# Opening the product of w3 and w_out2 with three row blocks, and taking the norms' roots with ln and exp

## Chip, cores and metric

The kernel runs on one core of a Trainium2 chip. The metric is the device time of one execution in microseconds (us), the median over the runs shown.

## What is computed

Attention over 4 batches of 12 heads (448 positions, 64 wide), with q and k normalised by the root of their mean square, feeds two feed-forward blocks. The second block multiplies its gated activations by `w3` and then by `w_out`:

```python
def rmsnorm(x, g):
    rms = np.sqrt(np.mean(x * x, axis=-1, keepdims=True) + 1e-06)
    return x / rms * g
...
h = x @ w_in; x = np.maximum(h, 0.0) ** 2 @ moe_w_out      # first block, cut
...
a = x @ w1
b = x @ w2
h = a * b @ w3
return (h @ w_out).astype(np.float32)
```

Tokens: 1792; model width 768; widths 2048 in the first block and 1024 in the second. The weights come as float64, the rest as float32.

## The kernel before

**Heads and fill.** The main loop (line 676) goes through the 48 heads, one to four steps of attention work per head: scores (`stage_qk`, line 513), exponentials (`stage_exp`, 529), transposes (`stage_t`, 562), product with v (`stage_v`, 614), and preparation of later heads (`head_prep`, 474; `group_prep`, 437, once for every four heads). Between them `fill(n)` (line 648) draws about n matmuls from a generator of matrix work, six times a head. While the 12 heads of batch 0 run, the generator is `gen_w3o` (line 272): it multiplies w3 by w_out2 ahead of time, so that the second block needs one product fewer. Its 384 matmuls are spread evenly over 13 heads, 29.5 each (line 677). After that the generator is `gen_moe` for the batch just finished.

**The product.** `gen_w3o` goes through eight row blocks `ic` of w3, each for two halves of w_out2's columns (384 each). For one row block and half it adds up eight steps `jc`, three matmuls each (`mm3`, line 260: high times high, high times low, low times high part) in one accumulator of the three PSUM tiles "mm" (line 95), which ScalarE then copies out (line 287) to one of two tiles "osb" for a store to DRAM (line 289). The first row block needs all 8 blocks of w_out2's first half, then all 8 of its second half; these stay in SBUF (tiles "x", "act" and "x2") for all later row blocks.

**Units.** Every weight block is a unit, in the order of the list `units` (lines 121 to 141): a block of w_out2 is 128x384, half a row block of w3 is 128x512. The order is: first half of w3 row block 0, w_out2 half 0 blocks 0 to 3, second half of row block 0, w_out2 half 0 blocks 4 to 7, w_out2 half 1, and then the other row blocks. `advance` (line 240) takes each unit through these steps, a few units ahead of its use: load of the float64 words into one of four "raw64" tiles by SyncE's queue (line 180), high word by ScalarE (line 194), low word by GpSimd or ScalarE (lines 198 and 200), joining to float32 by VectorE (line 207), rounded high part by ScalarE (line 106), low part by GpSimd or VectorE (line 114).

**Norms.** `rsqrt` (line 425) takes an inverse root on VectorE: an integer estimate (line 428) and three rounds of three small instructions (lines 432 to 434). It is called three times for the first group of four heads and once for each of the other 11 groups.

**Order.** The program's order is a priority: a planner in the compiler sorts the instructions of every engine by it and by estimated times, and each engine, SyncE's queue of loads included, then goes through its list in order. In the opening that list on SyncE has the first group's loads with units 0 and 1 among them (`load_group`, lines 396 to 403), then q of head 1, then (by `load_head(2)`) q of head 2, v, and k and q of the second group.

Of the kernel before, what the change touches and what calls it, by code (L numbers as in the profile page):

```python
# [8 lines left out]
F32 = mybir.dt.float32  # L9
F32R = mybir.dt.float32r  # L10
# [4 lines left out]
ALU = mybir.AluOpType  # L15
# [14 lines left out]
def attention_moe_kernel(  # L30
# [22 lines left out]
    NE = w_out.shape[0] // 4  # L53
    KF = w_out.shape[2] // 64
    NJ = w1.shape[0] // 2
    NIC = w3t.shape[0] // 2
    HC = KX * 128 // 2
    ENGS = {"v": nc.vector, "g": nc.gpsimd}
    KCS = ((0, 128), (128, 128), (256, 128), (384, 64))
# [61 lines left out]
    units = []  # L121
    wo_at, w3_at = {}, {}

    def add_wo(half, g):
        for j in range(NIC // 2):
            jc = g * NIC // 2 + j
            wo_at[half, jc] = len(units)
            units.append((wo2[jc, half], None))

    def add_w3(i):  # L130
        w3_at[i] = len(units)
        units.append((w3t[i], None))

    add_w3(0)
    add_wo(0, 0)
    add_w3(1)
    add_wo(0, 1)
    add_wo(1, 0)
    add_wo(1, 1)
    for i in range(2, 2 * NIC):  # L140
        add_w3(i)
    U0 = len(units)
    wo_units = set(wo_at.values())
    def two_first(n, on=True):
# [72 lines left out]
    def split_hi(i):  # L217
        n = units[i][0].shape[-1]
        if i in wo_units:
            k = pos["wo"]  # L220
            pos["wo"] += 1
            p, nm = (xp, "x") if k < 2 else ((actp, "act") if k < 10 else (x2p, "x2"))
            t = p.tile([128, 2, S], F32R, name=nm, tag=nm)
        else:
            t = hlp.tile([128, 2, 512], F32R, name="hl", tag="hl")
        copy_on("a", t[:, 0, :n], raws[i][:, :n])
        hls[i] = t
# [27 lines left out]

    def use(u):
        advance(u)
        return hls.pop(u).rearrange("p a (k m) -> p a k m", m=128)

    def mm3(ps, w, wk, x, i, n):  # L260
        last = n - 1
# [4 lines left out]
    def hl_pair(t, n=S):  # L266
        return (t[:, 0, :n], t[:, 1, :n])
# [2 lines left out]
    wo = {}  # L270

    def gen_w3o():
        for ic in range(NIC):
            ws = None
            for half in range(2):
                ps = ps_mm.tile([128, 512], F32, name="mm", tag="mm")
                for jc in range(NIC):
                    if ws is None or jc * 2 // NIC >= len(ws):
                        ws = (ws or []) + [use(w3_at[2 * ic + len(ws or [])])]
                    if ic == 0:  # L280
                        advance(wo_at[half, jc])
                        wo[half, jc] = hls.pop(wo_at[half, jc])
                    w = ws[jc * 2 // NIC]
                    mm3(ps[:, :HC], w, jc % (NIC // 2), hl_pair(wo[half, jc], HC), jc, NIC)
                    yield 3
                o = t2.tile([128, S], F32, name="osb", tag="osb")
                copy_on("a", o[:, :HC], ps[:, :HC])
                k, c = divmod(ic, NIC // 2)
                nc.sync.dma_start(
                    out=w3o.rearrange("(e k) p (c m) -> e k p c m", k=2, m=128)[half * 3:half * 3 + 3, k, :, c, :]  # L290
                    .rearrange("e p m -> p e m"),
                    in_=o[:, :HC].rearrange("p (e m) -> p e m", m=128),
                )


    xs = {}
# [128 lines left out]
    def rsqrt(y, x):  # L425
        t = small.tile([P, 2, GH * C], F32, name="nt", tag="nt")
        t = t[:, :x.shape[1], :x.shape[2]]
        nc.vector.tensor_scalar(
            out=y.bitcast(I32), in0=x.bitcast(I32), scalar1=-0.5, scalar2=1597463007.0, op0=ALU.mult, op1=ALU.add
        )  # L430
        for _ in range(3):
            nc.vector.tensor_tensor(out=t, in0=y, in1=y, op=ALU.mult)
            nc.vector.scalar_tensor_tensor(out=t, in0=t, scalar=-0.5, in1=x, op0=ALU.mult, op1=ALU.mult)
            ins = nc.vector.scalar_tensor_tensor(out=y, in0=t, scalar=1.5, in1=y, op0=ALU.add, op1=ALU.mult)
        return ins.ins

    def group_prep(g):
# [220 lines left out]
    MOE = 3 * (NFC * KX + 2 * NE * KF + 2 * NJ * KX + NE * NIC)  # L658
    W3O = 3 * 2 * NIC * NIC

    nc.sync.dma_start(out=g_sb, in_=g_in)
    load_group(0)
    load_head(1)
    make_identity(nc, ident)
    nc.vector.tensor_copy(out=ident_r, in_=ident)
    nc.vector.scalar_tensor_tensor(
# [7 lines left out]
    start_fill(gen_w3o(), W3O)  # L674
    first.close()
    for h in range(NH + 1):
        n = W3O / ((H + 1) * 6) if h <= H else MOE / (H * 6)
        load_head(h + 3)
        load_v(h + 1)
        if h % GH == 0:  # L680
            load_group(h // GH + 1)
        stage_qk(h, 0)
        fill(n)
        stage_exp(h, 0)
        if h % H != 1:
            stage_x(h - 2)
        stage_t(h - 1, 0)
        stage_t(h - 1, 1)
        fill(n)
        stage_lo(h - 1)  # L690
        if h < NH:
            v_prep(h)
        fill(n)
        stage_k(h + 1)
        stage_t(h - 1, 2)
        stage_t(h - 1, 3)
        fill(n)
        stage_lo(h - 1)
        stage_qk(h, 1)
        fill(n)  # L700
        stage_exp(h, 1)
        fill(n)
        stage_v(h - 1)
        if h % GH == 1:
            group_prep(h // GH + 1)
        head_prep(h + 2)
        if h and h % H == 0:
            fill(1e9)
            stage_x(h - 1)
            start_fill(gen_moe(h // H - 1), MOE)  # L710
# [57 lines left out]
```

## Time and profile before

| | us |
|---|---|
| median of 3 runs | 1234.7 (1232.09 to 1235.27) |
| the profiled execution | 1234.55 |
| its span in the profile | 1232.8 |
| TensorE matmul busy (PE) | 1160.9, 94% |
| GpSimd busy (POOL) | 781.3, 63% |
| ScalarE busy (ACT) | 728.5, 59% |
| VectorE busy (DVE) | 709.7, 58% |

PE is the matmul side of TensorE and PEld its weight loads; SP is SyncE, whose queue starts the loads, and SPq its queue. Times in the rows are us from the start of the span. A line number is that of the instruction in the kernel; L106 and L114 are the helpers that copy and subtract, so there the names of the tiles tell what is done.

### The profile page before, as it was taken

How to read it: one execution, taken by the hardware profiler on the slowest of the kernel's cores; microseconds unless marked ns; L12 is line 12 of the kernel's file. 1: busy time of each engine (PE TensorE's matmuls, PEld its weight loads, DVE VectorE, ACT ScalarE, POOL GpSimd, SP SyncE). 2: the span in 40 equal slices, each digit the busy share in tenths (PEclk: the TensorE clock that was granted, in tenths of full speed). 3: DMA queues.
4: the chain of work that ended last, by engine and by line, in shares of the span. 5: the costliest groups of instructions: out<-in, count | busy, mean ns of one | idle time of the engine just before them, and what ended most of it. 6: DMA issues, size and time to landing. Idle time of an engine off the chain costs nothing.

```text
span 1232.8 us, 18950 instructions
## 1 busy us (share of the span) xinstructions
PE 1160.9 (94%) x6192; PEld 1049.3 (85%) x6192; DVE 709.7 (58%) x1314; ACT 728.5 (59%) x1553; POOL 781.3 (63%) x772
## 2 busy tenths in 40 slices
PE   3789999998989899999999999999999999999998
PEld 2578888886878789998998998999999999999998
DVE  6699879768978774646567555655664421012100
ACT  5889876767657565656645555656545554343342
POOL 5875534655676655766776764856766556678673
PEclk9999999999998999999999999999999999999999
DMA  7774557888888755555535455544544443333342
GB/s 218 244 238 151 165 146 226 276 283 264 251 264 257 234 180 179 146 148 145 151 118 161 139 169 158 143 142 127 154 123 120 138 138 113 107 116 102 104 125 75
DMA packets 111347, 207.63 MB, mean 168 GB/s; under 512 B 12208, under 2 KB 66704, under 8 KB 111248
## 3 DMA queue, kind: packets, MB, share of 16 engines
q1 hardware_dynamic: 107792, 200.92, 54.0%
q10 hardware_dynamic: 3456, 5.51, 1.2%
q8 instruction: 49, 0.80, 0.3%
q14 instruction: 50, 0.41, 0.1%
HBM read 149.95 MB, written 27.53 MB: 144 GB/s over the span
## 4 chain that ended last, share of the span: by engine, by line
PE 60%; DMA 4%; DVE 2%; POOL 2%; ACT 1%; issue 1%; SPq 0%; DVEq 0%; POOLq 0%; ACTq 0%
PE mm L262 17%; PE mm L263 17%; PE mm L264 17%; PE kv L622 3%; PE pt L570 3%; DMA raw<-w 2%; DMA pw<-p 2%; PE sc L525 1%; PE sc L524 1%; POOL hl L114 1%; DVE raw L207 1%; PE kv L508 1%; PE mm L611 0%; ACT p L543 0%; POOL x L114 0%
## 5 line engine op out<-in xcount | busy, mean ns | idle before, releaser
L114 POOL TENSOR_TENSOR hl<-raw,hl 128x384 fp32r<-128x384 f32 (+1 forms) x383 | 446.4, 1169 | 258.5 <-ACT hl L106 253.3
L106 ACT ACTIVATE hl<-raw 128x384 fp32r<-128x384 f32 (+1 forms) x416 | 233.7, 564 | 147.6 <-PE mm L264 85.6
L263 PE MATMUL mm<-x,hl 128*128 128x448 f32 (+1 forms) x832 | 306.2, 368 | 8.6 <-POOL x L114 8.6
L262 PE MATMUL mm<-x,hl 128*128 128x448 f32 (+1 forms) x832 | 310.5, 373 | 3.8 <-ACT x L106 1.8
L264 PE MATMUL mm<-x,hl 128*128 128x448 f32 (+1 forms) x832 | 305.7, 367 | 4.5 <-POOL hl L114 2.6
L263 PE MATMUL mm<-act,hl 128*128 128x448 f32 (+1 forms) x640 | 234.4, 366 | 3.3 <-POOL act L114 3.2
L262 PE MATMUL mm<-act,hl 128*128 128x448 f32 (+1 forms) x640 | 236.9, 370 | 0.0
L264 PE MATMUL mm<-act,hl 128*128 128x448 f32 (+1 forms) x640 | 233.6, 365 | 0.7 <-DVE hl L114 0.7
L543 ACT ACTIVATE p<-sc,nb,rr 112x448 f32<-112x448 f32 x192 | 137.4, 719 | 86.4 <-DVE nb L527 83.0
L263 PEld LDWEIGHTS mm<-x,hl 128*128 128x128 f32 x832 | 158.1, 190 | 22.1 <-POOL x L114 10.2
L264 PEld LDWEIGHTS mm<-x,hl 128*128 128x128 f32 x832 | 158.2, 190 | 19.0 <-POOL hl L114 4.0
L262 PEld LDWEIGHTS mm<-x,hl 128*128 128x128 f32 x832 | 157.9, 190 | 18.5 <-ACT x L106 3.3
L526 DVE TENSOR_REDUCE nb<-sc 112x1 f32<-112x448 f32 x192 | 113.1, 615 | 35.6 <-PE sc L525 34.3
L263 PEld LDWEIGHTS mm<-act,hl 128*128 128x128 f32 x640 | 121.0, 189 | 14.3 <-POOL act L114 4.8
L264 PEld LDWEIGHTS mm<-act,hl 128*128 128x128 f32 x640 | 120.9, 189 | 10.6 <-DVE hl L114 1.1
L262 PEld LDWEIGHTS mm<-act,hl 128*128 128x128 f32 x640 | 121.0, 189 | 9.4
L114 DVE TENSOR_TENSOR ptr<-pt,ptr 128x448 fp32r<-128x448 f32 x144 | 87.1, 619 | 72.0 <-ACT ptr L106 71.4
L200 POOL TENSOR_SCALAR raw<-raw 128x384 uint32<-128x384 uint16 (+1 forms) x110 | 82.1, 747 | 73.0 <-DMA raw<-w_in 18.8
L207 DVE SCALAR_TENSOR_TENSOR raw<-raw 128x384 uint32<-128x384 uint32 (+1 forms) x120 | 84.8, 711 | 39.8 <-POOL hl L114 25.2
L194 ACT ACTIVATE raw<-raw 128x384 f32<-128x384 f32 (+1 forms) x120 | 70.5, 597 | 53.9 <-DMA raw<-w 18.0
L114 POOL TENSOR_TENSOR act<-gf,act 128x448 fp32r<-128x448 f32 x80 | 97.4, 1218 | 7.2 <-DVE gf L334 3.0
L334 DVE TENSOR_TENSOR gf<-mm,r 128x448 f32<-128x448 f32 x64 | 39.8, 621 | 94.4 <-ACT r L330 93.9
(82 smaller groups left out, 1588.7 us busy)
## 6 DMA issues: line engine op xcount, KB each, us to landing
pw<-p SPq DMA_DIRECT2D x72, 392.0 KB, 4.3
raw<-f_in SPq DMA_DIRECT2D x96, 192.0 KB, 2.4
raw<-f_out SPq DMA_DIRECT2D x72, 256.0 KB, 2.7
raw<-f SPq DMA_DIRECT2D x96, 192.0 KB, 2.4
raw<-w_in SPq DMA_DIRECT2D x32, 384.0 KB, 4.5
raw<-w_out SPq DMA_DIRECT2D x24, 512.0 KB, 6.1
raw<-w SPq DMA_DIRECT2D x32, 384.0 KB, 4.9
raw<-w3o SPq DMA_DIRECT2D x48, 256.0 KB, 2.7
```

The costliest lines, as they stand in the source:

```text
L106: nc.scalar.activation(out=out, in_=in_, func=AF.Copy)
L114: e.tensor_tensor(out=out, in0=in0, in1=in1, op=ALU.subtract)
L194: nc.scalar.activation(out=hi, in_=hi, func=AF.Prelu, scale=2.0**-112, alpha=-(2.0**32))
L200: nc.gpsimd.tensor_scalar(out=t[:, :n, 0], in0=low, scalar1=2.0**-13, scalar2=2.0**-14 - 0.5, op0=ALU.mult, op1=ALU.add)
L207: nc.vector.scalar_tensor_tensor(out=f[:, :n].bitcast(U32), in0=t[:, :n, 1], scalar=3, in1=t[:, :n, 0], op0=ALU.logical_shift_left, op1=AL ...
L262: nc.tensor.matmul(ps, w[:, 0, wk, :], x[0], start=(i == 0), stop=False)
L263: nc.tensor.matmul(ps, w[:, 0, wk, :], x[1], start=False, stop=False)
L264: nc.tensor.matmul(ps, w[:, 1, wk, :], x[0], start=False, stop=(i == last))
L334: nc.vector.tensor_tensor(out=gf, in0=ps, in1=r, op=ALU.mult)
L526: nc.vector.tensor_reduce(out=nb[:, j:j + 1], in_=o[j], axis=AX.X, op=ALU.max, negate=True)
L543: nc.scalar.activation(out=p, in_=o[j], func=AF.Exp, scale=d["rq"][:, c:c + 1], bias=nb[:, j:j + 1], accum_out=sm[:, i, c:c + 1],)
L570: nc.tensor.transpose(to[:kn, c * P:(c + 1) * P], d["p"][c][:, k0:k0 + kn], one)
```

## The change

The product's units are cut and ordered anew, the generator opens with three row blocks at once, heads 0 and 1 get 27 matmuls each and the later ones 30, units 2 and 3 are loaded right after q of head 1, and `rsqrt` corrects the integer estimate y by exp(-0.5 ln(x y y)) on ScalarE, whose table of functions is chosen by name at the start.

```diff
-    NIC = w3t.shape[0] // 2
+    NIC = w3t.shape[0]
+    NR = 3
...
+    CUTS = [(0, 3, 6, 8)] * (NR - 1) + [(0, 4, 8)] * (NIC - NR + 1)
+    for jc in range(NIC):
+        for ic in range(NR):
+            if jc in CUTS[ic][:-1]:
+                add_w3(ic, jc, CUTS[ic][CUTS[ic].index(jc) + 1])
+            if ic == 0:
+                add_wo(0, jc)
+    for jc in range(NIC):
+        add_wo(1, jc)
+    early = {w3_at[ic, jc][0] for ic in range(NR - 1) for jc in range(NIC)}
+    for ic in range(NR, NIC):
+        for a, b in zip(CUTS[ic], CUTS[ic][1:]):
+            add_w3(ic, a, b)
...
-            p, nm = (xp, "x") if k < 2 else ((actp, "act") if k < 10 else (x2p, "x2"))
+            p, nm = (actp, "act") if k < 8 else ((x2p, "x2") if k < 14 else (xp, "x"))
             t = p.tile([128, 2, S], F32R, name=nm, tag=nm)
+        elif i in early:
+            t = xp.tile([128, 2, S], F32R, name="x", tag="x")
...
     def gen_w3o():
+        ws = {}
+
+        def rows(ics, half):
+            pss = [ps_mm.tile([128, 512], F32, name="mm", tag="mm") for _ in ics]
+            for jc in range(NIC):
+                for ic, ps in zip(ics, pss):
+                    u, i = w3_at[ic, jc]
+                    if u not in ws:
+                        ws[u] = use(u)
                     if ic == 0:
                         advance(wo_at[half, jc])
                         wo[half, jc] = hls.pop(wo_at[half, jc])
+                    mm3(ps[:, :HC], ws[u], i, hl_pair(wo[half, jc], HC), jc, NIC)
+                    if jc == NIC - 1:
+                        o = t2.tile([128, S], F32, name="osb", tag="osb")
+                        copy_on("a", o[:, :HC], ps[:, :HC])
...
                     yield 3
...
+        for half in range(2):
+            yield from rows(range(NR), half)
+        for ic in range(NR, NIC):
+            for half in range(2):
+                yield from rows([ic], half)
...
-        for _ in range(3):
-            nc.vector.tensor_tensor(out=t, in0=y, in1=y, op=ALU.mult)
-            nc.vector.scalar_tensor_tensor(out=t, in0=t, scalar=-0.5, in1=x, op0=ALU.mult, op1=ALU.mult)
-            ins = nc.vector.scalar_tensor_tensor(out=y, in0=t, scalar=1.5, in1=y, op0=ALU.add, op1=ALU.mult)
+        nc.vector.tensor_tensor(out=t, in0=y, in1=y, op=ALU.mult)
+        nc.vector.tensor_tensor(out=t, in0=t, in1=x, op=ALU.mult)
+        nc.scalar.activation(out=t, in_=t, func=AF.Ln)
+        nc.scalar.activation(out=t, in_=t, func=AF.Exp, scale=-0.5)
+        ins = nc.vector.tensor_tensor(out=y, in0=t, in1=y, op=ALU.mult)
...
+    nc.scalar.preload_act_table_set("natural_log_exp_and_others")
     nc.sync.dma_start(out=g_sb, in_=g_in)
     load_group(0)
     load_head(1)
+    load_to(3)
...
-        n = W3O / ((H + 1) * 6) if h <= H else MOE / (H * 6)
+        n = (9 * NR if h < 2 else (W3O - 18 * NR) / (H - 1)) / 6 if h <= H else MOE / (H * 6)
...
-        "w3t": units(w3.T, 4),
+        "w3t": units(w3.T, 8),
```

## Rows read from the trace of the kernel before

**Rows 1.** The page's 40 equal slices: TensorE's busy tenths in each.
```profile
PE   3789999998989899999999999999999999999998
```

**Rows 2.** Windows by head: length, busy us of each engine (instructions), clock, DMA, GB/s.
```profile
0.00:11.60 11.60, 0.73 (x4) 0.56 (x4) 5.90 (x22) 6.01 (x10) 4.12 (x11) 1.00 0.78 237
11.60:33.00 21.40, 11.33 (x33) 7.55 (x34) 15.10 (x38) 12.21 (x26) 16.28 (x19) 1.00 0.66 200
33.00:56.20 23.20, 15.75 (x69) 11.57 (x67) 15.78 (x25) 17.67 (x40) 19.46 (x20) 0.93 0.81 263
56.20:76.70 20.50, 16.48 (x98) 14.72 (x97) 19.02 (x36) 17.26 (x35) 14.78 (x13) 1.00 0.75 229
76.70:97.30 20.60, 19.78 (x123) 17.09 (x122) 20.21 (x35) 19.63 (x43) 15.65 (x19) 1.00 0.62 198
97.30:178.00 80.70, 75.39 (x465) 68.12 (x464) 69.43 (x150) 65.44 (x145) 38.74 (x50) 1.00 0.53 158
178.00:340.00 162.00, 147.07 (x792) 130.65 (x793) 137.52 (x254) 112.16 (x242) 92.73 (x101) 0.99 0.81 257
340.00:1232.00 892.00, 874.40 (x4620) 799.02 (x4618) 426.69 (x760) 478.06 (x1018) 579.54 (x541) 0.99 0.49 147
```

**Rows 3.** TensorE's waits, 11 to 100: us in total, times, longest.
```profile
PE mm L263 <- POOL x L114: 7.3, 4, 2.9
PE sc L524 <- ACT p L543: 3.4, 1, 3.4
PE mm L263 <- POOL act L114: 3.2, 4, 1.7
PE pt L570 <- DVE nt L432: 2.7, 1, 2.7
```

**Rows 4.** Timeline of TensorE: second matmul of the product's first two steps.
```profile
15.43 0.69 PE L263 MATMUL mm<-x,hl 128*128 128x384 f32 x1 [1.39 <-POOL x L114]
...
29.95 0.69 PE L263 MATMUL mm<-x,hl 128*128 128x384 f32 x1 [2.91 <-POOL x L114]
```

**Rows 5.** Timeline of SyncE's queue, 0 to 20: start, us, line, what.
```profile
4.47 2.85 SPq L414 DMA_DIRECT2D qt<-q_t  x2
...
14.96 1.37 SPq L180 DMA_DIRECT2D raw<-wo  x3
```

**Rows 6.** Windows, 25 to 58: PE, PEld, DVE, ACT, POOL as in rows 2.
```profile
25.00:58.00 33.00, 20.44 (x81) 15.07 (x82) 21.51 (x35) 25.16 (x57) 27.82 (x29) 0.95 0.74 234
```

**Rows 7.** The same stretch for line 194 alone: ScalarE's busy us (units).
```profile
25.00:58.00 33.00, 9.10 (x16) 0.95 0.74 234
```

**Rows 8.** Line 262, 0 to 97.3: count, ns min/median/max, first to last start.
```profile
L262 PE MATMUL mm<-x,hl x26: 334/339/690, 13.4 to 94.2; 128*128 128x384 f32 x26
L262 PE MATMUL mm<-act,hl x26: 333/338/522, 30.8 to 97.0; 128*128 128x384 f32 x26
```

**Rows 9.** ScalarE's work on units (tile raw), 0 to 97.3, columns as in rows 8.
```profile
L194 ACT ACTIVATE raw<-raw x29: 524/563/687, 7.2 to 87.4; 128x384 f32<-128x384 f32 x16, 128x512 f32<-128x512 f32 x13
...
L198 ACT ACTIVATE raw<-raw x9: 534/560/667, 23.5 to 79.6; 128x384 uint32<-128x384 uint16 x5, 128x512 uint32<-128x512 uint16 x4
...
L106 ACT ACTIVATE act<-raw x8: 508/523/524, 27.6 to 42.1; 128x384 fp32r<-128x384 f32 x8
```

**Rows 10.** One of three like instructions of the roots (tile nt), 0 to 97.3.
```profile
L432 DVE TENSOR_TENSOR nt<-rr x12: 150/176/946, 4.6 to 72.9; 112x4 f32<-112x4 f32 x6, 112x24 f32<-112x24 f32 x3, 112x32 f32<-112x32 f32 x3
```

**Rows 11.** ScalarE's longest wait, 0 to 97.3, columns as in rows 3.
```profile
ACT p L543 <- DVE nb L527: 6.3, 3, 5.7
```

**Rows 12.** Groups by line, 0 to 97.3: count, busy us, mean ns, idle before.
```profile
L543 ACT ACTIVATION_READ_ACCUMULATOR p<-sc,nb,rr 112x1 f32 x19 | 3.7, 194 | 0.0
...
L450 ACT ACT_TABLE_LOAD x1 | 1.3, 1283 | 0.7 <-PEq L755 0.7
```

**Rows 13.** Stores of the product (line 289): from issue to landing.
```profile
DMA to landing us min/median/max: 2.1/3.4/5.3
```

More of the change, by code (lines that the diff above doesn't have):

```diff
@@ L122, in attention_moe_kernel, with add_wo, add_w3 @@
     wo_at, w3_at = {}, {}
[L124 to L141, printed above, removed]
+    def add_wo(half, jc):
+        wo_at[half, jc] = len(units)
+        units.append((wo2[jc, half], None))
+    def add_w3(ic, a, b):
+        for jc in range(a, b):
+            w3_at[ic, jc] = (len(units), jc - a)
+        units.append((w3t[ic][:, a * 128:b * 128], None))
+    CUTS = [(0, 3, 6, 8)] * (NR - 1) + [(0, 4, 8)] * (NIC - NR + 1)
[11 more added lines that the diff above has]
+            add_w3(ic, a, b)
     U0 = len(units)
@@ L257, in use @@
         advance(u)
-        return hls.pop(u).rearrange("p a (k m) -> p a k m", m=128)
+        return hls.pop(u)[:, :, :units[u][0].shape[-1]].rearrange("p a (k m) -> p a k m", m=128)
     def mm3(ps, w, wk, x, i, n):
@@ L272, in gen_w3o @@
     def gen_w3o():
[L273 to L279, printed above, removed]
+        ws = {}
[6 more added lines that the diff above has]
+                        ws[u] = use(u)
                     if ic == 0:
@@ L282, in gen_w3o @@
                         wo[half, jc] = hls.pop(wo_at[half, jc])
-                    w = ws[jc * 2 // NIC]
-                    mm3(ps[:, :HC], w, jc % (NIC // 2), hl_pair(wo[half, jc], HC), jc, NIC)
-                    yield 3
[L286 to L293, printed above, removed]
+                    mm3(ps[:, :HC], ws[u], i, hl_pair(wo[half, jc], HC), jc, NIC)
+                    if jc == NIC - 1:
+                        o = t2.tile([128, S], F32, name="osb", tag="osb")
+                        copy_on("a", o[:, :HC], ps[:, :HC])
+                        k, c = divmod(ic, NIC // 2)
+                        nc.sync.dma_start(
+                            out=w3o.rearrange("(e k) p (c m) -> e k p c m", k=2, m=128)
+                            [half * 3:half * 3 + 3, k, :, c, :].rearrange("e p m -> p e m"),
+                            in_=o[:, :HC].rearrange("p (e m) -> p e m", m=128),
+                        )
+                    yield 3
+        for half in range(2):
[3 more added lines that the diff above has]
+                yield from rows([ic], half)
     xs = {}
```

## Prediction

> **What bounds the kernel now.** I read the page's slices first, then windows cut at the first scores matmul of heads 0, 1, 2, 3, 5 and 12, then TensorE's waits in the opening, and last the engines that those waits name. The slices show TensorE at nine tenths nearly everywhere but in the first two, at 3 and 7 [rows 1]. The windows say the same in us [rows 2]: from 340 on it is busy for 874.4 of 892, so there is next to nothing to win there. Heads 5 to 11 take 80.7, or 11.5 each, with TensorE busy for 75.4 (93%). Heads 3 and 4 take 20.6, 10.3 each, with TensorE, VectorE and ScalarE all at 95% or more. Heads 0, 1 and 2, though, take 21.4, 23.2 and 20.5, about twice a later head, and TensorE is busy there for 43.6 of 65.1. Against 10.3 a head that is 34 us too much: the most that a better opening could ever give.
>
> What TensorE waits for there is weights [rows 3]: 7.3 and 3.2 us for low parts that GpSimd writes into the tiles x and act, which are w_out2 blocks, against 3.4 for a score tile and 2.7 for VectorE's roots. The product's first step has its low part at 15.43, the second only at 29.95 [rows 4]. From 25 to 58 GpSimd is busy for 27.8 of 33 [rows 6] while 16 units pass their first step [rows 7], which is 2.06 us a unit, against three matmuls that such a unit feeds in the first row block. In that row block the product needs a new unit for every step, so it runs at the pace of units, and the attention work that stands behind it in TensorE's list waits with it.
>
> **Units in the opening.** Counting by the code, head 0 now draws 29.5 matmuls, which need 12 units, and head 1 seven more. After the change heads 0 and 1 draw 27 each: three steps of nine matmuls, with three w_out2 blocks and three pieces of w3 each, so 6 and 6 units. At 2.06 us these are 12.4 us a head, where 12 were 24.7, more than the 21.4 that head 0 takes now. Supply then no longer sets the length of a head, and the next limit is the work of ScalarE and VectorE themselves.
>
> So I price the stretch up to head 5 by those two. ScalarE works 72.8 there (the sum of the first five windows), VectorE 76.0 [rows 2]. Now 29 units have begun by then, 16 of 384 columns and 13 of 512 [rows 9]. After it: 16 blocks of w_out2, three row blocks of 1024 columns, and three units ahead of 512, so 2048 columns fewer, four wide units' worth. On ScalarE a unit costs 0.563 + 0.560 x 9/29 + 0.523 = 1.26 [rows 9], so 5.0 less. VectorE's joins of these four I leave out. They are not saved, they come later.
>
> **Roots.** Each call loses nine small VectorE instructions and gets three back, so six fewer; 12 of line 432 are four calls up to 97.3, so 24 x 0.176 = 4.2 off VectorE [rows 10]. ScalarE gets eight: no row shows ln or exp over 4 to 32 elements, so between 0.194, the read of one element [rows 12], and 0.523 for 384 [rows 9]; 32 are nearer to one, so 8 x 0.194 = 1.6, at most 4.2. The chain gets shorter in count but crosses to ScalarE and back; what it holds up now is ScalarE's exponentials in head 0 (5.7 in one wait, [rows 11]) and the 2.7 of TensorE. I give it no term of its own: what it frees is part of the share below.
>
> **Sum of the opening.** ScalarE: 72.8 - 5.0 + 1.6 = 69.4, of which 6.0 lie in the first 11.6, which I leave as they are: 63.4 remain. VectorE: 76.0 - 4.2 = 71.8, less 5.9: 65.9 remain. VectorE is the heavier. At the share of heads 3 and 4 (20.21 of 20.6, 98%) this takes 67, at that of heads 0 to 2 (49.9 of 65.1, 77%) 86. With supply in time the opening is more like heads 3 and 4, but the first head still has to wait for its loads, so I take 90%: 73.2, and head 5 begins at 84.8 instead of 97.3. That is **12.5 less**; 18.5 and about zero are the ends.
>
> **What is given back.** By 97.3 there are 52 first matmuls of a step [rows 8], so about 154 of the 384. After the change head 5 begins at 27 + 27 + 3 x 30 = 144, so ten come later, where TensorE is the bound, at 874.4/4620 = 0.189 each [rows 2]: **1.9 more**. The four units' 5.0 on ScalarE go into heads 5 to 11, beside 65.4 of 80.7: hidden behind TensorE's 93%; 5.0 if that cover is gone. Two calls of the roots there and eight later are 6 x 0.176 = 1.1 each off an engine that waits for TensorE anyway: nothing, at most 2.
>
> **Edits that I cost at nothing.** Units 2 and 3 go ahead of q of head 2, v and the second group on SyncE's queue. That queue stands from about 5 to 7 us anyway, since two loads of q fill 4.47 to 7.32, the second of them held for a free tile; units 2 to 4 leave only at 14.96 [rows 5]. Two issues cost under 1 us in that hole, but their 0.92 MB take 3.9 us at the 237 GB/s of the first window [rows 2]. What stands behind is v of head 0 and the second group, needed only once probabilities exist and one head later; if that cover fails, 3.9. The earlier landing is what lets nine matmuls run before 20 instead of three, and is in the share. The three open accumulators take all three tiles, so at the end of each half the third copy waits for the first of two osb tiles to be stored, 3.4 to landing [rows 13]; attention matmuls cover it; if they don't, 2 x 3.4 = 6.8.
>
> **Total.** 1234.55 - 12.5 + 1.9 = 1223.95, against the profiled execution, whose span is 1232.8 with 1.75 around it; it lies 0.15 under the median of the runs shown, which I ignore. I say 1224.
>
> **Rival 1: given back.** The matmuls and pieces pushed out of heads 0 and 1 fall into heads 2 to 4 and on, where ScalarE and VectorE are already full, and the half changes cost their 6.8. For it: 95 and 98% in heads 3 and 4. Against it: the sum of work before head 5 falls, it does not move within it. Then 12.5 - 1.9 - 6.8 - 2.5 (half of the 5.0) leaves 1.3: about 1233.
>
> **Rival 2: slower, by table loads.** Now one table load serves the whole kernel, 1.283 us [rows 12]. If ln were not served by the same table as the exponentials, copies and the first step of units, each root would load twice on ScalarE, between VectorE's product and its last one, 2.57 a call. Six calls lie in batch 0's heads, where little hides it: 15.4, and 1224 + 15.4 = 1239.4; later ones lie beside TensorE. It takes at least (1238.4 - 1224)/2.57 = 5.6 calls on the path, so all six, before the kernel is slower. Against it: the change names one table at the start, and the row shows that squares, copies and exponentials have lived with one load.
> The Trainium skill (ScalarE: Activation LUTs, "Table sets: the hidden batching unit") lists that set as holding both exp and ln, with the cheap functions in every set, and by "What ACT_TABLE_LOAD costs" a switch is about 2.66 us with its drain. By that price, an estimate, the six calls would come to 1224 + 6 x 2 x 2.66 = 1256 if the set did not hold; if it holds, no term changes. The load alone took 1.283 in the row; the drain no run here shows.
>
> **Rival 3: more.** VectorE reaches the 98% of heads 3 and 4 from head 0 on, and the shorter roots free 2 more later: 1234.55 - 18.5 + 1.9 - 2 = 1216, or a little less if the first 11.6 shrink too, for the piece of w3 in front is 384 columns instead of 512: 1214.
>
> **A risk inside the forecast.** ScalarE goes through its list in order, so an ln placed too early holds everything behind it until VectorE's product is there, as the 5.7 us wait for nb does now [rows 11]. Two hand-overs a call over batch 0's six calls, at the 0.52 of an ordinary instruction [rows 9], would be 6; that leads toward rival 1 and is in its chance.
>
> **Chances.** Forecast 0.67 (own range 1217 to 1230), rival 1 0.18 (1230 to 1237), rival 2 0.07, rival 3 0.06, anything else 0.02, split evenly. A measurement of this kernel tells 0.3%, or 3.7 us, from no change: under 1231.0 is faster, over 1238.4 slower. Faster: 0.65 of the forecast's 0.67, rival 3's 0.06 and 0.03 of rival 1, so 0.74; same: 0.02 + 0.15 + 0.01 = 0.18; slower: 0.08. The range is 1214 to 1234: it leaves out rival 2, a part of rival 1 and a little below, under 0.2.
>
> **What would show it.** Right: the windows of heads 0 to 2 shrink to 15 to 19 us each, head 5 begins near 85, the waits of line 263 on x and act fall under 4 us in sum, SyncE's queue issues units 2 and 3 before 7 us, heads 5 to 11 take 80 to 84, and all behind moves by the same amount. ScalarE shows one table load. Wrong: head 5 begins after 93, or heads 5 to 11 take over 88, or TensorE waits for the copies of the accumulators by over 3 us twice, or there are many table loads.

## The result: 1244.8 us, 0.8% slower than before

The changed kernel took 1244.8 us (1242.6 to 1247.2) against 1234.7 for the kernel before on the same chip: a ratio of 1.0084 with an interval of 1.0062 to 1.0106. The forecast was 1224. Its profiled execution took 1242.63 with a span of 1240.8, which is 8.0 more than the span before.

First the page's slices of the changed kernel (busy tenths, and the granted clock in tenths):

```profile
PE   3789889998889899999999999999999999999998
PEclk9799999999999999999999999999999999999999
```

Against [rows 1] only slices 5, 6 and 11 differ (one slice is 31 us), and only downward: most was decided before 190 us. Next the windows cut at its own first scores matmuls of heads 0, 1, 2, 3, 5 and 12, the columns as in [rows 2]:

```profile
0.00:13.50 13.50, 0.73 (x5) 0.58 (x5) 5.79 (x19) 6.89 (x15) 4.38 (x12) 1.00 0.79 236
13.50:30.20 16.70, 8.24 (x29) 5.71 (x29) 8.79 (x18) 7.87 (x19) 14.14 (x19) 0.95 0.62 189
30.20:55.10 24.90, 19.73 (x79) 17.31 (x80) 18.88 (x32) 20.45 (x46) 13.49 (x15) 0.71 0.70 227
55.10:71.80 16.70, 12.38 (x58) 10.06 (x58) 10.73 (x22) 11.24 (x27) 13.16 (x18) 0.88 0.45 136
71.80:98.50 26.70, 23.77 (x145) 20.80 (x143) 22.55 (x40) 23.33 (x53) 18.91 (x20) 1.00 0.76 239
98.50:187.20 88.70, 79.09 (x471) 70.70 (x470) 73.09 (x140) 69.71 (x155) 46.18 (x55) 0.98 0.56 161
```

Head 5 begins at 98.5 instead of 97.3; 84.8 was forecast. Heads 5 to 11 take 88.7 instead of 80.7. Yet the work fell: over the first five rows ScalarE is busy for 69.8 (forecast 69.4, before 72.8) and VectorE for 66.7 (forecast 71.8, before 76.0). What did not come is the share: from 13.5 on VectorE is busy for 60.9 of 85.0, 72%, and ScalarE for 62.9, 74%, not 90%.

The table shows the start of some heads in the traces (first scores matmul). "One row", "two rows" and so on are experiments below. The last columns are the length from head 8 to 13 and the median time; the kernel before, measured again beside each group of them, stood at 1234.7 to 1236.9, so times are compared by their ratios to it.

| kernel | head 3 | head 5 | head 8 | head 13 | head 24 | 8 to 13 | time |
|---|---|---|---|---|---|---|---|
| before | 76.7 | 97.3 | 131.6 | 188.9 | 462.7 | 57.2 | 1234.7 |
| changed | 71.8 | 98.5 | 132.9 | 197.1 | 471.1 | 64.2 | 1244.8 |
| roots only | 74.1 | 94.5 | 131.5 | 191.2 | 461.7 | 59.7 | 1232.7 |
| one row | 76.2 | 97.9 | 130.7 | 191.8 | 462.3 | 61.1 | 1235.7 |
| two rows | 76.7 | 105.6 | 137.1 | 195.3 | 467.9 | 58.1 | 1241.0 |
| even pace | 77.4 | 99.3 | 136.4 | 199.5 | 471.1 | 63.1 | 1244.2 |
| blocks only | 70.0 | 96.2 | 130.3 | 202.2 | 475.8 | 71.9 | 1248.5 |
| w_in late | 71.5 | 99.8 | 132.9 | 186.7 | 460.9 | 53.8 | 1234.9 |
| w_in late, before | 78.1 | 98.7 | 134.9 | 187.8 | 465.7 | 52.9 | 1242.3 |
| w_in row 5 | 71.6 | 99.9 | 133.0 | 190.2 | 463.3 | 57.1 | 1235.7 |
| no low word | 66.2 | 91.6 | 127.1 | 187.5 | 461.9 | 60.4 | 1239.5 |
| units as float32 | 56.3 | 81.3 | 115.9 | 175.3 | 450.0 | 59.4 | 1221.7 |

Of the 8.2 us that the changed kernel is behind at head 13, 1.2 come up to head 5, none from 5 to 8 (34.4 in both) and 7.0 from head 8 to 13. From head 24 to the end both need 770.

TensorE's waits in the opening of the changed kernel (11 to 100, columns as in [rows 3]; the wait from the start to the first transpose at 11.9 is left out):

```profile
PE kv L524 <- POOL khl L115: 4.8, 1, 4.8
PE mm L271 <- POOL hl L115: 4.4, 2, 3.1
PE mm L269 <- ACT osb L107: 3.8, 2, 2.0
PE sc L540 <- ACT p L559: 3.7, 3, 2.3
PE mm L269 <- ACT act L107: 1.4, 2, 0.9
PE mm L270 <- POOL act L115: 1.2, 1, 1.2
```

The waits for low parts of w_out2 fell from 7.3 and 3.2 to 1.2, as they should. In their place stand the next head's k (4.8), the low part of a w3 piece (4.4) and the hand-over of accumulators (3.8). From 13.5 to 98.5 TensorE is idle for 20.9 (64.1 of 85.0 busy): 7.3 of it for parts of units (hl, act and 0.3 for x), 3.8 for accumulators, nearly all the rest for the attention's own steps.

### The profile page after: what moved, and what is told of

The parts are those of the page before. It is cut to its first block, busy times and chain, and to the rows that moved or that the text cites. A ratio compares the mean times of both kernels' runs of the same rounds, so it can differ in the third digit from the quotient of the medians.

```text
span 1240.8 us, 18885 instructions
## 1 busy us (share of the span) xinstructions
PE 1164.1 (94%) x6192; PEld 1051.7 (85%) x6192; DVE 684.9 (55%) x1231; ACT 732.5 (59%) x1586; POOL 788.0 (64%) x776
## 4 chain that ended last, share of the span: by engine, by line
PE 65%; DMA 11%; DVE 9%; ACT 7%; POOL 5%; issue 4%; SPq 1%; DVEq 0%; ACTq 0%; POOLq 0%
PE mm L269 18%; PE mm L271 18%; PE mm L270 18%; PE kv L638 3%; PE pt L586 3%; ACT p L559 2%; DMA pw<-p 2%; DMA raw<-w_in 2%; DVE raw L212 2%; PE sc L540 2%; PE sc L541 2%; POOL hl L115 2%; DVE nb L542 1%; DMA raw<-w_out 1%; DMA raw<-w 1%
## 5 line engine op out<-in xcount | busy, mean ns | idle before, releaser
L107 ACT ACTIVATE hl<-raw 128x384 fp32r<-128x384 f32 (+1 forms) x412 | 231.2, 564 | 148.9 <-PE mm L271 88.2
L269 PE MATMUL mm<-x,hl 128*128 128x448 f32 (+1 forms) x816 | 303.2, 372 | 2.4 <-ACT osb L107 1.8
L271 PE MATMUL mm<-x,hl 128*128 128x448 f32 (+1 forms) x816 | 299.3, 367 | 2.3 <-POOL hl L115 1.3
L270 PE MATMUL mm<-x,hl 128*128 128x448 f32 (+1 forms) x816 | 298.8, 366 | 1.3 <-POOL x L115 1.3
L271 PE MATMUL mm<-act,hl 128*128 128x448 f32 (+1 forms) x624 | 228.6, 366 | 5.9 <-POOL hl L115 5.9
L269 PE MATMUL mm<-act,hl 128*128 128x448 f32 (+1 forms) x624 | 231.7, 371 | 0.0
L270 PE MATMUL mm<-act,hl 128*128 128x448 f32 (+1 forms) x624 | 228.1, 366 | 0.0
L271 PEld LDWEIGHTS mm<-x,hl 128*128 128x128 f32 x816 | 154.1, 189 | 17.0 <-POOL hl L115 2.7
L269 PEld LDWEIGHTS mm<-x,hl 128*128 128x128 f32 x816 | 154.1, 189 | 16.0 <-ACT osb L107 2.1
L270 PEld LDWEIGHTS mm<-x,hl 128*128 128x128 f32 x816 | 154.2, 189 | 13.6 <-POOL x L115 1.6
L271 PEld LDWEIGHTS mm<-act,hl 128*128 128x128 f32 x624 | 118.0, 189 | 16.3 <-POOL hl L115 7.0
L205 POOL TENSOR_SCALAR raw<-raw 128x384 uint32<-128x384 uint16 (+2 forms) x111 | 81.2, 731 | 78.0 <-DMA raw<-w_in 34.7
L269 PEld LDWEIGHTS mm<-act,hl 128*128 128x128 f32 x624 | 118.2, 189 | 9.3
L270 PEld LDWEIGHTS mm<-act,hl 128*128 128x128 f32 x624 | 118.2, 190 | 8.9
L212 DVE SCALAR_TENSOR_TENSOR raw<-raw 128x384 uint32<-128x384 uint32 (+2 forms) x122 | 84.3, 696 | 55.6 <-POOL hl L115 32.2
L540 PE MATMUL sc<-kt,qh 128*112 128x448 f32 x192 | 76.3, 397 | 23.6 <-ACT p L559 22.6
L199 ACT ACTIVATE raw<-raw 128x384 f32<-128x384 f32 (+2 forms) x122 | 70.4, 591 | 46.5 <-DMA raw<-w 16.7
```

Source lines behind the costliest of these rows:

```text
L107: nc.scalar.activation(out=out, in_=in_, func=AF.Copy)
L199: nc.scalar.activation(out=hi, in_=hi, func=AF.Prelu, scale=2.0**-112, alpha=-(2.0**32))
L205: nc.gpsimd.tensor_scalar(out=t[:, :n, 0], in0=low, scalar1=2.0**-13, scalar2=2.0**-14 - 0.5, op0=ALU.mult, op1=ALU.add)
L212: nc.vector.scalar_tensor_tensor(out=f[:, :n].bitcast(U32), in0=t[:, :n, 1], scalar=3, in1=t[:, :n, 0], op0=ALU.logical_shift_left, op1=AL ...
L269: nc.tensor.matmul(ps, w[:, 0, wk, :], x[0], start=(i == 0), stop=False)
L270: nc.tensor.matmul(ps, w[:, 0, wk, :], x[1], start=False, stop=False)
```

## Experiments

### The parts of the change

**roots only**: the kernel before, with the new `rsqrt` and the table chosen by name.

```diff
...
+        nc.scalar.activation(out=t, in_=t, func=AF.Ln)
+        nc.scalar.activation(out=t, in_=t, func=AF.Exp, scale=-0.5)
...
+    nc.scalar.preload_act_table_set("natural_log_exp_and_others")
```

> The kernel before with the new roots alone (ln and exp on ScalarE, the table named at the start); product and loads as before. If the crossing of the roots from VectorE to ScalarE and back is what costs, in the place and the size of the whole loss: 1241 to 1245, with the loss again in heads 8 to 11. If the product's new order is what costs: 1232 to 1236, and the marks of the heads within 2 us of the kernel before up to head 12. If the early load alone costs: also 1232 to 1236.

**blocks only**: the changed kernel with the old roots and without the early load.

```diff
-        nc.scalar.activation(out=t, in_=t, func=AF.Ln)
-        nc.scalar.activation(out=t, in_=t, func=AF.Exp, scale=-0.5)
...
-    nc.scalar.preload_act_table_set("natural_log_exp_and_others")
...
-    load_to(3)
```

> The kernel before with the new order of the product alone (three row blocks open at once, new cuts, new pace), old roots, units 2 and 3 loaded at their old place. If the product's order costs: 1239 to 1245. If the roots cost: 1222 to 1236, at best the 11 us that the prediction gave to the opening. If the early load is what spoils the opening: head 5 begins before 92 us.

**no early load**: only the last of these lines goes.

```diff
-    load_to(3)
```

> The changed kernel without the early load of units 2 and 3. If that load holds up the first k and q and so everything (first scores at 13.5 instead of 11.6): first scores at 11.5 to 12, and 1236 to 1241. If it is not the cause: 1242 to 1247, and the first scores may come earlier without any gain behind them.

**old roots**: the changed kernel with the old three rounds on VectorE and no table named, the early load kept.

```diff
-        nc.scalar.activation(out=t, in_=t, func=AF.Ln)
-        nc.scalar.activation(out=t, in_=t, func=AF.Exp, scale=-0.5)
...
-    nc.scalar.preload_act_table_set("natural_log_exp_and_others")
```

> The changed kernel with the old roots on VectorE and the old table. If the roots cost: 1232 to 1238. If the product's order or the early load costs: 1241 to 1247, and the loss in heads 8 to 11 stays.

Measured, as ratios to the kernel before: roots only 0.9973 (0.9959 to 0.9987), blocks only 1.0098 (1.0074 to 1.0121), no early load 1.0060 (1.0037 to 1.0083), old roots 1.0081 (1.0056 to 1.0107). So the new order of the product costs about 12 us by itself. The roots give 3.7 on the old order; on the new one 5.1 without the early load (the intervals just overlap) and nothing that can be told with it. By the ratios the early load is between 2.1 won (old roots against blocks only) and 3.0 lost (changed against no early load), and the intervals overlap. Two expectations missed: blocks only lies above its 1239 to 1245, and with the roots only heads 1, 2, 3 and 5 moved by 2.6 to 7.0 us from the kernel before (head 1 at 26.0 instead of 33.0), not by less than 2.

### Pace, or rows that are open at once?

**even pace**: all 13 heads draw 29.5 matmuls again.

```diff
-        n = (9 * NR if h < 2 else (W3O - 18 * NR) / (H - 1)) / 6 if h <= H else MOE / (H * 6)
+        n = W3O / ((H + 1) * 6) if h <= H else MOE / (H * 6)
```

> The changed kernel with one line put back: every one of the first 13 heads gets 29.5 matmuls, as before, instead of 27, 27 and then 30; units, row blocks, early load and roots as changed. Theory A, density: the new order needs 24 units for its first 144 matmuls of the half-accounts (up to head 5) where the old one needed 18 for 48, so the loads and steps of units go on at full density to head 5, the lead that the kernel before had built by head 3 (109 matmuls done, against 83) is not there, and heads 8 to 12 pay for it. The pace then hardly matters: 1241 to 1246. Theory B, phase: with 27 and 30 the pair of unit steps that each 48 matmuls bring falls into another place of the head than before, behind the head's loads of q, v and the group's k in SyncE's list; with the even pace it falls as before, heads 8 to 13 go back from 64 us to about 57, and the time is 1234 to 1238.

**two rows** and **one row**: the same with one more number.

```diff
-    NR = 3
+    NR = 2
```

> The changed kernel with two row blocks at once instead of three, and the even pace of 29.5 matmuls a head. Its first two row blocks need 16 blocks of w_out2 and 5 units of w3 for 96 matmuls of the list, so the dense stretch ends in head 3 instead of head 5. Theory A, density: the time lies between the kernel with the old product order and the new roots (1232.7) and the changed one (1244.8), 1236 to 1241, and the loads of w_in begin near 97 us, as before, instead of 104 to 106. Theory B, phase: as the run with the even pace and three row blocks, within 2 us.

> The changed kernel with one row block at once and the even pace of 29.5 matmuls a head: the order of the units is then that of the kernel before, and what is left of the change is the assignment of units to tiles, the early load of units 2 and 3 and the roots. Theory A (the rows that are open at once cost the time): it stands with the kernel of old order and new roots, 1231 to 1235, and heads 8 to 13 take 57 to 60 us, as in the two kernels with one row block (57.3, 59.7) and the one with two (58.1), against 63 to 72 in the seven with three. Rival (the tile assignment or the early load costs it): 1240 to 1245 and over 62 us in heads 8 to 13.

Even pace took 1244.2 and 63.1 us from head 8 to 13: the theory of the phase fell. Two rows took 1241.0 (ratio 1.0042), one row 1235.7 (0.9990, interval 0.9971 to 1.0008): the time goes with the number of rows (between two and three the intervals overlap), and neither the other tiles nor the early load costs it, up to the 0.2% by which one row stands behind the roots alone. Three parts missed. One row needed 61.1 from head 8 to 13, more than the 60 expected, though less than the 63 to 72 of the three-row kernels; its time lies 0.7 over the 1231 to 1235. And with two rows the w_in loads began at 107.7, not near 97, and still heads 8 to 13 took 58.1: a late start of these loads is not by itself the loss. Two rows loses in the opening instead (head 5 at 105.6).

### Why the opening gains nothing

**q later**: the loads of q for heads 2 and 3 go behind v and the second group.

```diff
-    load_head(2)
     head_prep(1)
...
-        load_head(h + 3)
+        if h:
+            load_head(h + 3)
...
+        if h == 0:
+            load_head(2)
...
+        if h == 0:
+            load_head(3)
         stage_k(h + 1)
```

> The changed kernel with the loads of q for heads 2 and 3 put behind the loads of v and of the second group in the program's order (head 3's also behind the first fill), so that SyncE's queue is no longer held from 8.7 to 16.6 us by a load that waits for a free q tile. Theory: the hold makes units 4 and later come 5 to 7 us late and takes back what the new order should gain in the opening. Expected: units 4 and 5 issued at 12 to 14 us instead of 18.4, head 2 near 50 instead of 55, head 5 near 93 instead of 98.5. If heads 8 to 12 then still lose 8 to 10 us, the total is 1239 to 1241. Rival: supply after unit 4 is bound by the steps of a unit on the engines and not by its load: head 5 stays within 2 us of 98.5 and the time at 1243 to 1246.

The reason for it was this stretch of SyncE's queue in the changed kernel (start, us, line, what), where a load of q waits for a free tile from 8.7 to 16.6 with the next units behind it:

```profile
4.94 1.53 SPq L185 DMA_DIRECT2D raw<-w3t  x2
6.76 0.46 SPq L429 DMA_DIRECT2D qt<-q_t  x1
8.37 0.33 SPq L437 DMA_DIRECT2D v<-v_in  x1
16.58 0.33 SPq L429 DMA_DIRECT2D qt<-q_t  x1
...
18.42 0.85 SPq L185 DMA_DIRECT2D raw<-wo  x2
```

In the run units 4 and 5 left at 14.7, but head 5 began at 98.2 and the time was 1246.3. The rival held, with a time 0.3 over its range: what comes 4 us sooner waits for something else.

**no low word**: the low-word step of the product's units is left out (a zero word is joined instead), so the products lack the low words.

```diff
+        if i < U0:
+            return
         if low_eng[i % len(low_eng)] == "a":
...
-            out=f[:, :n].bitcast(U32), in0=t[:, :n, 1], scalar=3, in1=t[:, :n, 0],
+            out=f[:, :n].bitcast(U32), in0=t[:, :n, 1], scalar=3,
+            in1=t[:, :n, 0] if i >= U0 else zero[:, 0:1].to_broadcast([128, n]),
```

> The changed kernel without the low-word step of the product's 34 units (it leaves out the low word of w3 and w_out2, so about 25 steps of 0.6 to 0.9 us on GpSimd and 9 of 0.7 us on ScalarE are gone; the join adds a zero word in its place). The forecast took the opening as bound by the work of ScalarE and VectorE at 90% of the time. Theory of order: work is not the limit, the engines wait for each other in their lists; taking some 20 us of GpSimd's and 6 us of ScalarE's work out of the opening and the stretch to head 5 moves head 5 by no more than 4 us (94.5 to 98.5). Rival, work: GpSimd's low words are on the path of nearly every unit, and head 5 comes 8 to 15 us earlier, at 84 to 90.

Head 5 came at 91.6, 6.9 earlier: between the two bands, so neither theory alone. The time was 1239.5 (ratio 1.0030, interval 1.0009 to 1.0050).

**units as float32**: the product's units are loaded as float32 words of q, so the product has other operands and all steps on words are gone; the splits stay.

```diff
+            if i < U0:
+                m = min(n, S)
+                nc.sync.dma_start(out=t[:, :m], in_=q_t[0, i % H][:, :m])
...
```

> The changed kernel whose 34 units of the product are loaded as float32 words of q instead of float64 words of w3 and w_out2 (it leaves the product's real operands and all steps on their words out: 34 high words on ScalarE, 25 low on GpSimd, 9 on ScalarE, 34 joins on VectorE; the splits into high and low parts stay). If the units' steps set the opening, head 5 comes at 75 to 85 us instead of 98.5, and the forecast's 84.8 was out of reach with the word steps in place. If the attention's own chain and the splits set it, head 5 stays over 90.

Head 5 at 81.3, in the first band: the units' steps on words are worth 17.2 us of the opening. Here is the stretch from the first scores to head 5, first of the changed kernel, then of this one (PE, PEld, VectorE, ScalarE, GpSimd):

```profile
13.50:98.50 85.00, 64.12 (x308) 53.87 (x308) 60.95 (x111) 62.89 (x144) 59.70 (x70) 0.88 0.65 206
```

```profile
13.70:81.30 67.60, 56.42 (x305) 50.76 (x304) 52.31 (x92) 51.34 (x116) 47.19 (x55) 0.90 0.73 206
```

There is less work, and it is packed little better: VectorE's share goes from 72% to 77%, ScalarE's from 74% to 76%. At the old share VectorE's 52.3 would take 73.0, so by this estimate 12 of the 17 us are work that is gone and 5 are waits. 90% does not come with the word steps gone either. (The loads of these units move half the bytes in this run too; what that contributes was not separated.)

### Heads 8 to 12

The first theory came from the trace of the changed kernel at 126 to 139. SyncE's queue issues w_in loads late, behind a load of v that waits for its tile:

```profile
119.91 0.33 SPq L429 DMA_DIRECT2D qt<-q_t  x1
125.92 0.33 SPq L437 DMA_DIRECT2D v<-v_in  x1
126.35 1.13 SPq L185 DMA_DIRECT2D raw<-w_in  x2
```

GpSimd stands at the low word of such a block until it has landed, and the next head's k and a w3 unit's low part stand behind it:

```profile
131.66 0.99 POOL L205 TENSOR_SCALAR raw<-raw 128x384 uint32<-128x384 uint16 x1 [3.16 <-DMA raw<-w_in]
132.73 0.62 POOL L496 TENSOR_TENSOR kx<-kn,rr 112x256 f32<-112x256 f32 x1
133.31 1.15 POOL L115 TENSOR_TENSOR x<-xf,x 128x448 fp32r<-128x448 f32 x1
134.54 0.55 POOL L205 TENSOR_SCALAR raw<-raw 128x384 uint32<-128x384 uint16 x1
135.17 1.30 POOL L115 TENSOR_TENSOR hl<-raw,hl 128x512 fp32r<-128x512 f32 x1
```

VectorE stands 3.81 us at the join of a w_in unit until that low part frees a raw tile, with the maxima of the scores (nb) and the sum of the last product with v (xf) behind it:

```profile
136.50 0.56 DVE L212 SCALAR_TENSOR_TENSOR raw<-raw 128x384 uint32<-128x384 uint32 x1 [3.81 <-POOL hl L115]
136.98 0.49 DVE L568 TENSOR_SCALAR sm<-sm 112x8 f32<-112x8 f32 x1
137.38 0.61 DVE L542 TENSOR_REDUCE nb<-sc 112x1 f32<-112x448 f32 x1
137.91 0.19 DVE L570 RECIPROCAL rs<-sm 112x8 f32<-112x8 f32 x1
138.02 0.56 DVE L646 TENSOR_TENSOR xf<-kv,vt 64x448 f32<-64x448 f32 x1
```

And TensorE waits for that sum: its tile must be free before the next k can be transposed.

```profile
138.73 0.50 PE L524 MATMUL kv<-ident_r,khl 112*128 112x112 f32 x4 [2.21 <-DVE xf L646]
```

**word 2**: the words are split two units ahead instead of three.

```diff
-    WORD_AHEAD = 3
+    WORD_AHEAD = 2
```

> The changed kernel with the step that splits a unit's words taken two units ahead instead of three (one number), so that GpSimd's low word stands later in its in-order list than the landing of its load. Theory C, ring: heads 8 to 12 are long because GpSimd stands 11 us longer than before (16.6 instead of 5 to 6 us from 128 to 188) at a low word whose w_in block has not landed, and kx, the next head's k, stands behind it. With the step later these waits fall under 8 us in that stretch, heads 8 to 13 take 57 to 60 us instead of 64, and the time is 1236 to 1241. Rival, density (theory A): the waits only change their place, since the units are late as such; the time stays within 2 us of 1244.8 or rises, because the opening has one unit less ahead.

It took 1244.6, with 63.0 from head 8 to 13. GpSimd's waits for w_in blocks fell only from 16.6 to 11.3 between 120 and 195, and the two-row kernel has 15.9 of them without the loss: GpSimd's waits alone are not it.

**w_in late**, and the same in the kernel before as a control: the w_in loads wait for the product's last accumulator, so no step of theirs lies in heads 6 to 11.

```diff
             t = t3.tile([128, 512, 2], U32, name="raw64", tag="raw64", bufs=4)
+            if U0 <= i < U0 + 4:
+                nc.vector.tensor_copy(out=t[:, 0, 0:1], in_=osb_last[0][:, 0:1].bitcast(U32))
...
+        last = U0 - 1 if u < U0 else NU - 1
-        while pos["lo"] <= min(u + SPLIT_AHEAD, NU - 1):
+        while pos["lo"] <= min(u + SPLIT_AHEAD, last):
...
```

> The changed kernel, in which the loads of w_in (the first weights after the product) wait for the product's last accumulator, by a copy of one column into each of the four raw64 tiles; so no step of a w_in unit lies in heads 6 to 11. Theory D: in heads 8 to 12 the attention's steps stand in the in-order lists behind steps of w_in units whose loads land late (VectorE's join 3.8 us, GpSimd's low word 3.2 us at 131 to 136). Then heads 8 to 13 fall from 64 to 57 us or less; what follows in heads 13 and 14 is longer, since w_in then comes late, so the total says little, 1238 to 1260. Rival: the stretch is long by the attention's own chain, and stays at 62 us or more without the w_in steps.

> The control: the same hold of the w_in loads in the kernel before. Heads 8 to 13 take 57.3 us there with the w_in steps among them; without them 53 to 57. If both kernels come to the same length, the w_in steps are what sets them apart; if the changed one stays over 5 us longer, it is something else.

This tells where the loss of heads 8 to 12 comes from. Without w_in steps the two kernels need 53.8 and 52.9 from head 8 to 13, against 64.2 and 57.2 with them: the same steps cost 10.4 in the new order and 4.3 in the old (11.7 and 2.5 if the stretch is taken from head 5). The changed kernel fell to 1234.9 (0.9994, interval 0.9976 to 1.0011), the kernel before rose to 1242.3 (1.0055, 1.0035 to 1.0074). The totals are only in part explained. In both, head 13 then takes longer (30.5 and 28.8 us against 21.7 and 21.1). The changed kernel has made that up by head 24 (460.9 against 471.1), the kernel before has not (465.7 against 462.7), and its trace is 4.8 us longer behind head 24 as well, which is not explained.

**w_in row 5**, **w_in row 6** and **roots, w_in row 6** let the loads in again earlier, after half 1 of that row block.

```diff
...
+                        if (ic, half) == (5, 1):
+                            osb_last.append(o)
...
```

> The same with row block 5 (about 150 us). Presence: heads 10 to 12 pay, head 13 at 190 to 194, 1236 to 1242. Crowding: head 13 at 187 to 190 and 1226 to 1234.

> The changed kernel, in which the w_in loads wait for the accumulator of row block 6 (half 1, due at about 165 us) instead of for the last one at 187 us. If any w_in step among the attention's costs, heads 8 to 11 are as without them (head 11 near 164 instead of 172.6) and the loss comes back in heads 11 and 12: 1233 to 1238. If it is crowding at 126 to 141, the stretch stays short throughout (head 13 at 187 to 189) and the wait of head 13 to 14 for w_in (30 us with the later hold, 22 in the changed kernel) falls as well: 1226 to 1232.

> The kernel before with the new roots (1232.7) and the hold of the w_in loads for row block 6. In the kernel before the full hold took 4.4 us off heads 8 to 13 and gave 7.7 back at heads 13 to 14. With the earlier release: 2 to 4 us won in heads 8 to 13 and at most 2 given back, 1229 to 1234; if the loss at head 13 stays, 1236 to 1240.

Row 5 took 1235.7 (1.0001, interval 0.9987 to 1.0016) with head 13 at 190.2, between what presence and crowding were expected to give. The stretch from 131 to 188, of the kernel before, the changed one and that with row 5:

```profile
131.00:188.00 57.00, 53.94 (x333) 48.74 (x331) 47.57 (x113) 43.83 (x98) 21.18 (x29) 1.00 0.54 154
```

```profile
131.00:188.00 57.00, 47.99 (x281) 42.56 (x279) 43.40 (x83) 39.10 (x89) 26.79 (x33) 0.97 0.54 158
```

```profile
131.00:188.00 57.00, 53.46 (x330) 48.32 (x329) 49.43 (x107) 46.64 (x106) 27.36 (x37) 1.00 0.69 203
```

GpSimd does as much there with row 5 as in the changed kernel (27.4 and 26.8), DMA more, and 12 w_in units pass their high-word step against 8, while TensorE gets 330 matmul records in instead of 281. So it is not the amount of w_in work but where it stands in the lists. Row 6 missed: heads 8 to 13 took 58.1, as with row 5, but 3 us were lost again between heads 13 and 24 (277.0 against 274.0 in the changed kernel) and head 5 had come 1.2 later than with row 5; it came to 1243.5 (1.0062). With the old order it missed too: 1240.5, with head 13 at 188.0 and head 24 already behind at 463.6. So what a hold gains in heads 8 to 13 shows in the total for row 5 and for the full hold of the changed kernel only.

### A version that beats both

**roots, w_in row 5** joins what helped; **roots again** repeats the roots alone beside it.

> The kernel before with the new roots, in which the w_in loads wait for the accumulator of row block 5 (about 150 us). In the three-row kernel this hold shortened heads 8 to 13 from 64 to 57 us; here they take 59.7 us without it. Expected: 56 to 58 us there, no loss at head 13, 1229 to 1233. If the old order has nothing to gain, since its w_in steps come spread out already, 1232 to 1238.

> The kernel before with the new roots alone, again: 1231 to 1235, ratio 0.996 to 0.999.

The first took 1234.8 (0.9987, interval 0.9973 to 1.0000), the second 1232.6 (0.9971, 0.9955 to 0.9987). The first missed its 1229 to 1233: the stretch from head 8 to 13 shrank to 57.8 as expected, but the total did not follow. The old order has little to gain from the hold. The roots alone, twice 0.3% faster, are the best of the kernels that do the whole computation.

## Why the prediction was wrong

Measured and forecast time lie 20.8 apart. At head 5 the traces are 13.7 behind the forecast (98.5 against 84.8), and heads 5 to 11 take 88.7, where 80 to 84 were named. Both are signs that I had given for being wrong (head 5 after 93, heads 5 to 11 over 88).

**Units in the opening: the step that failed first.** "Supply then no longer sets the length of a head" does not hold. Six units were forecast for head 0 and six for head 1. High-word steps (units) of the changed kernel by head:

```profile
0.00:13.50 13.50, 1.10 (x2) 1.00 0.79 236
13.50:30.20 16.70, 1.18 (x2) 0.95 0.62 189
30.20:55.10 24.90, 6.41 (x12) 0.71 0.70 227
55.10:71.80 16.70, 3.26 (x6) 0.88 0.45 136
71.80:98.50 26.70, 5.18 (x8) 1.00 0.76 239
```

Head 0's stretch passes two units and head 1's twelve, in 24.9 us: 2.08 each, where 2.06 was forecast. The product lies the same way: of the nine steps that each of these heads draws, 3 run in head 0's stretch and 17 in head 1's (first matmuls, line 269). What a head draws in the program is thus not what runs in its stretch. Nor was the count carried to head 5: 30 units begin before it against 29 [rows 9], fewer columns but as many steps. I had left out what heads 2 to 4 then need: 14 units, where 10 passed before.

The pace of 2.06 does not explain the whole opening, though. Heads 2 to 4 take 43.4 us for their 14 units, 3.1 each, and other orders passed the units of head 1 faster (two rows 16 in 27.9 us, one row 13 in 22.3).

**Sum of the opening: the 90%, mis-sized.** The share was 72%, below even the 77% of heads 0 to 2 before; the low end that I gave, about zero, is what came. Supply alone does not account for it: without the word steps the share is still only 77%, and of TensorE's 20.9 us of waits only 7.3 are for units. With the changed kernel's 61.0 of VectorE, 90% would have put head 5 at 81.2. That ScalarE's sum came out right (69.8 for 69.4) is luck: its steps on the units (tile raw) fell from 34.6 to 33.4, by 1.2 and not by 5.0, and 2.1 are squares of q and k (tile qn, 5.5 to 3.4) that lie behind head 5 now. VectorE was not the heavier engine either, with 61.0 against ScalarE's 62.9.

A slower TensorE is not the main cause: its granted clock was 0.71 through head 1, but with blocks only it was 1.00 in heads 0 and 1 and 0.90 in head 2, and head 5 still came at 96.2.

**Given back: mis-sized.** Head 5 began with 50 first matmuls of a step done instead of 52, so six matmuls come later: 6 x 0.189 = 1.1 instead of 1.9. But heads 5 to 11 did not hide what was left to them: 88.7 us against the 80 to 84 that I named. "Hidden behind TensorE's 93%" counted work, and the loss is order: TensorE is at 89% there, and the w_in steps that cost it 10.4 us stood in no term and no rival of mine. This was the second step that failed.

**Edits at nothing.** Units 2 and 3 left before 7 us, as forecast, and it gave nothing that can be told. Nine matmuls of the product were to run before 20 us; three did, as before. TensorE's list has head 1's k next, and its low part came only then:

```profile
16.02 0.52 PE L271 MATMUL mm<-act,x 128*128 128x384 f32 x1
21.34 0.73 PE L524 MATMUL kv<-ident_r,khl 112*128 112x112 f32 x4 [4.79 <-POOL khl L115]
```

The accumulators' hand-over cost 3.8 of TensorE's time in two waits of at most 2.0, between nothing and the 6.8; so rival 1's mechanism was there, but only as a part, and the time went 12 past its 1233.

**Roots: right.** Here are the lines of the new roots on ScalarE and the table load over the whole span of the changed kernel (busy, mean ns, idle before):

```profile
L449 ACT ACTIVATE nt<-nt 112x32 f32<-112x32 f32 (+2 forms) x14 | 3.1, 221 | 0.3
L448 ACT ACTIVATE nt<-nt 112x32 f32<-112x32 f32 (+2 forms) x14 | 3.1, 220 | 10.6 <-DVE nt L447 10.6
L677 ACT ACT_TABLE_LOAD x1 | 1.3, 1283 | 0.7 <-PEq L773 0.7
```

0.22 each, near the 0.194 that I took. The risk that I named is there as well: ln holds ScalarE's list for 10.6 us over 14 calls, and the change is still worth 0.3% on the old order. I had given the roots no term of their own.

**Rival 2: wrong mechanism.** The sign was its own, the cause was not: there is one table load, of 1.283 us. The Trainium skill (ScalarE: Activation LUTs, "Table sets: the hidden batching unit") has ln and exp in one set, and the trace agrees.

**What stays open.** Why w_in's steps fall worse with three rows than with one is not shown, nor what holds the engines at 72 to 77% in the opening beyond the waits named. The planner sorts every list anew after each edit: between heads 13 and 24 these kernels differ by 5 us though the program is the same there (270.5 with one row, 275.6 without the early load), so a few us of any single stretch can be the list and not the edit. What goes beyond that: the seven kernels with three rows, the whole computation and no hold need 63.0 to 71.9 from head 8 to 13, the three with the hold 53.8 to 58.1.

## What to carry to other kernels

When supply limits a stretch, count the units up to its end and not only in its first heads: moving their use about within it does not take any away. Check their pace in every part of it, too: here it went from 2.1 us a unit in one head to 3.1 in the next three. A share of busy time read from a good stretch is no price for another one whose engines wait for each other. And where in-order lists mix prefetch steps with a critical chain, ask of each list what stands behind a step whose load may land late: holding the prefetch back was worth 9 to 10 us in the changed kernel in two of three places, and nothing in the old order, so it has to be measured and not assumed.

## What the hardware showed that I had not expected

The granted clock fell behind a stretch of waits and made a loss larger. TensorE in three stretches of the changed kernel (busy, records, clock, DMA share, GB/s):

```profile
120.00:130.00 10.00, 9.73 (x63) 1.00 0.36 94
130.00:140.00 10.00, 6.47 (x40) 1.00 0.68 210
140.00:150.00 10.00, 9.52 (x46) 0.83 0.75 219
```

In the second stretch TensorE was busy for 6.5 of 10 us; in the third the clock is at 0.83 on average, a mix of 2.4 and 1.2 GHz. Like matmuls show both levels:

```profile
142.26 0.52 PE L269 MATMUL mm<-act,hl 128*128 128x384 f32 x1
142.58 0.52 PE L270 MATMUL mm<-act,hl 128*128 128x384 f32 x1
...
145.33 0.33 PE L270 MATMUL mm<-act,hl 128*128 128x384 f32 x1
145.50 0.33 PE L271 MATMUL mm<-act,hl 128*128 128x384 f32 x1
```

They start 0.32 us apart at the lower level and 0.17 at the higher. At 0.83 the 10 us lose about 1.7 us (an estimate, 10 x 0.17) that no row of waits shows. In the opening the clock was at 0.71 through head 1, where before it was at 0.93 [rows 2].
